# How v is loaded, how the last MLP group leaves, and who sets the order, in a fused attention and MLP kernel

## The chip, the cores and the metric

The kernel runs on one core of one Trainium2 chip. The core has a matrix engine (TensorE, PE in the profile; its weight loads are shown apart, as PEld), three engines for element work (VectorE or DVE, ScalarE or ACT, GpSimd or POOL), a SyncE (SP) that here only issues transfers, and 16 DMA engines. Each engine works through its own instructions strictly in the order in which they were written. ScalarE can issue transfers too, from a queue of its own. The metric is the device time of one execution, in microseconds (us); lower is better.

## The reference

```python
# q, k, v: (4 batches, 4 heads, 1088 tokens, 32);  S1, S2: (8, 32)
def phi(x):                               # 64 features of a token
    a = einsum('rd,bhsd->bhsr', S1, x);  b = einsum('rd,bhsd->bhsr', S2, x)
    return einsum('bhsi,bhsj->bhsij', a, b).reshape(..., 64)
kv  = einsum('bhsf,bhsd->bhfd', phi(k), v);   z = phi(k).sum(tokens)
att = einsum('bhsf,bhfd->bhsd', phi(q), kv) / (einsum('bhsf,bhf->bhs', phi(q), z) + 1e-6)
x   = att as 4352 tokens of 4 * 32 = 128 values
h   = x @ w_in                            # 128 -> 2048
out = (max(h, 0) + alpha * min(h, 0)) @ w_out    # 2048 -> 128, float32
```

## The kernel before

**Attention.** The 1088 tokens of a batch are taken so that partition-sized groups of 32 tokens have a stride of 34: token t * 34 + j stands in row t, block j, for 32 rows and 34 blocks. For keys and values the 34 blocks are dealt into four groups of at most nine that begin at blocks `K0 = (0, 9, 17, 25)`; group g sits on partitions 32g to 32g + 31 of `v_sb[b]`, and blocks that two groups share are left out of the later one (`w0 = g // 2`). One batch's v is loaded by four DMAs, one for each group (`l_v`, line 322): 32 partitions, all four heads, nine or eight blocks of 32 values.

For each batch, `keys` does: transpose k (L461), project it by S1 and S2 (L469, TensorE), transpose back (L476), multiply out the 64 features (L484, `phi`, four products, GpSimd or VectorE), the sum over tokens as a small Gram matrix (L499, then L506, L507 and L509) that goes into `Wq[b]` (L511), and the product with v (L519), copied (L523), transposed (L530) and copied (L532) into `kvw[b]`. L519 is the only reader of v.

Queries come in five units (`UNITS`): two for batch 0 (512 and 576 tokens), one for each other batch. A unit transposes q (L546), projects it and takes the denominator at once with `Wq[b]` (L555), transposes (L561), divides (L576 to L583), multiplies out the features (L590), transposes (L596), multiplies with `kvw[b]` (L610) and writes x, transposed and in bf16, to `xT` (L619).

**MLP.** `GROUPS` cuts the 4352 tokens into eight groups of 512 and a last one of 256. max(h, 0) + alpha * min(h, 0) is computed as (1 - alpha) * max(h, 0) + alpha * h, so that out = relu(h) @ ((1 - alpha) * w_out) + x @ W, with W = w_in @ (alpha * w_out), made once (transposes L430, scaling L438 or L441, products L448, copy L451). A group has 16 chunks: a product with `w_in` into a PSUM bank (L633), a relu into a buffer `rh` (L640 on ScalarE or L642 on VectorE), a product with `w_out` summed in PSUM bank O (L646); and one product with W (L653). The result stands by feature, tokens in columns; VectorE transposes it in blocks of 32 (L658), and four DMAs write 32 features each in runs of 128 bytes (L670). For the last group two of the four go out on ScalarE's queue.

**Order.** Each piece of work is an `op` with the engines that it may run on, an estimated duration, what it depends on and the buffers that it takes. At build time `schedule` picks, again and again, the ready op that its estimates let start first, ties by priority; `ORDER` overwrites the priorities of the first 200-odd ops. The order in which ops are picked is the order in which each engine runs. Where it expects TensorE to sit idle early on, it puts in products of zeros (`filler`, L382). Loads of batches 1 to 3 are held back by tiny writes on VectorE into the destination (`gate`, L356), after which SP may issue them.

SP issues at the start k0 (two DMAs), q0a, v0 (four), w_in (two), w_out (two). ScalarE issues S1 and S2 ("rows") and alpha, then loads its function table.

Of the kernel before, what the change touches and what calls it, by code (L numbers as in the profile page):

```python
# [12 lines left out]
BF16 = mybir.dt.bfloat16  # L13
# [15 lines left out]
SLACK = {"ACT": 140, "PE": 0, "DVE": 170}  # L29
# [3 lines left out]
ORDER = [  # L33
# [48 lines left out]
STICK = {"PE": 5000}  # L82


def schedule(ops, slots, filler=None):
# [4 lines left out]

    free_at = {"DVE": 830, "PE": 900, "POOL": 700, "ACT": 700}
    cfg, glued = "full", None
# [4 lines left out]
    def slot_free(s):  # L97
        h = holder[s]
        if h is None:
            return slot_at[s]  # L100
        if any(o.end is None for o in h.frees) or not h.frees:
            return None
        return max(o.end + 150 for o in h.frees)

    waits = {id(o): sum(d.end is None for d in o.deps) for o in ops}
    users = {}
    for o in ops:
        for d in o.deps:
            users.setdefault(id(d), []).append(o)
    ready = [o for o in ops if waits[id(o)] == 0]  # L110
    order = []
    while ready:
        best = None
        known = {}
        for o in ready:
            t0 = 0
            picks = []
            ok = True
            taken = set()
            for h in o.takes:  # L120
                for s in h.names:
                    if s not in known:
                        known[s] = slot_free(s)
                cand = sorted((known[s], s) for s in h.names if known[s] is not None and s not in taken)
                if len(cand) < h.n:
                    ok = False
                    break
                chosen = cand[:h.n]
                taken |= {s for _, s in chosen}
                picks.append([s for _, s in chosen])  # L130
                t0 = max([t0] + [t for t, _ in chosen])
            if not ok:
                continue
            for e, dur in o.eng.items():
                if e == "PE":
                    if glued is not None and o is not glued:
                        continue
                    if o.cfg != cfg:
                        dur += SWITCH
                    if free_at.get("PE", 0) < COLD and not o.warm:  # L140
                        dur *= 2
                t = max(t0, free_at.get(e, 0))
                if o.port and e in ("DVE", "POOL"):
                    t = max(t, free_at.get("PORT", 0))
                for d in o.deps:
                    t = max(t, d.end + (0 if d.on == e else d.lat if d.on == "DQ" else d.lat + SLACK.get(e, 0)))
                if e == "PE":
                    for i, (limit, at) in enumerate(have):
                        if issued + o.ni > limit:
                            t = max(t, have[i + 1][1])  # L150
                o_key = (t, o.prio, t + dur)
                if best is None:
                    best = []
                best.append((t, o.prio, t + dur, o, e, dur, picks))
        assert best, "no operation can start"

        t_first = min(b[0] for b in best)
        near = [b for b in best if b[0] <= t_first + 60]
        t, _, end, o, e, dur, picks = min(near, key=lambda b: (
            b[1] - (STICK["PE"] if b[4] == "PE" and b[3].cfg == cfg != "full" else 0), b[2]))  # L160
        if e == "PE" and filler and 4000 < free_at.get(e, 0) < FILL:
            each = 430 if free_at[e] < COLD else 215
            n = int((t - free_at[e] - 40) / each)
            idle = [s for s in FILL_BANKS if slot_free(s) is not None and slot_free(s) <= free_at[e]
                    and s not in sum(picks, [])]
            if n > 0 and idle:
                x = filler(n, idle[-1], each)
                x.behind = [f for f in holder[idle[-1]].frees] if holder[idle[-1]] else []
                x.end, x.on, x.took = free_at[e] + each * n, e, each * n
                order.append((free_at[e], e, x))  # L170
                slot_at[idle[-1]] = x.end
                holder[idle[-1]] = x.takes[0]
                issued += x.ni
                cfg = x.cfg
# [3 lines left out]
        if e == "PE":  # L178
            issued += o.ni
            cfg, glued = o.cfg, o.glue  # L180
            if issued > have[-1][0] - 256:
                have.append((have[-1][0] + 256, max(end, free_at.get("DQ", 0)) + 2600))
        for h, names in zip(o.takes, picks):
            h.got = names
            o.behind += [f for s in names if holder[s] for f in holder[s].frees]
            for s in names:
                holder[s] = h
        order.append((t, e, o))
        ready.remove(o)
        for u in users.get(id(o), ()):  # L190
            waits[id(u)] -= 1
            if waits[id(u)] == 0:
                ready.append(u)
# [5 lines left out]
def kernel(  # L199
# [12 lines left out]
    nc = tc.nc  # L212
# [511 lines left out]
```

## Time and profile before

| | us |
|---|---|
| median of three runs (105.97 to 108.0) | 106.73 |
| the profiled execution | 106.62 |
| its span, first to last instruction | 103.9 |
| TensorE busy in it | 96.5 |
| VectorE, ScalarE, GpSimd busy | 71.3, 71.3, 43.3 |
| first MLP product (L633) starts | 20.64 |
| last group's transpose (L658) starts | 100.18 |

A busy share is an average over the whole span, so the stages are looked at one by one: which engine a stage waits for last. In the lines of the timeline and of the groups stand the line of the code, the engine, the operation, the buffer written and those read, and how many instructions were taken together; times are microseconds from the span's start. In the chain that ended last, each piece is what released the next one. "SPq" and "ACTq" are the issuing of transfers by SP and ScalarE; "DMA" there is a transfer's way until it has landed. In a window's row stand, after its length, the busy times of PE, PEld, DVE, ACT and POOL with their instruction counts, the granted TensorE clock, the mean busy share of the 16 DMA engines and GB/s.

### The profile page before, as it was taken

What the parts mean: (1) busy time and instruction counts of PE and PEld (TensorE: products, weight loads), DVE (VectorE), ACT (ScalarE), POOL (GpSimd) and SP (SyncE); (2) the same over time, 40 slices, a digit from 0 to 9 for tenths busy, and PEclk for the clock granted to TensorE, in tenths of its full rate; (3) what the DMA queues carried; (4) which work ended last, traced back from release to release, by engine and by line L of the source; (5) the groups of instructions that cost most, each with busy time, mean ns of one, the idle gap of its engine ahead of it and who ended that gap; (6) DMA issues with size and microseconds to landing.
All of it is one profiled execution on the core that took longest, in us unless ns stands there. A gap on an engine that the chain in (4) does not pass through costs nothing.

```text
span 103.9 us, 3351 instructions
## 1 busy us (share of the span) xinstructions
PE 96.5 (93%) x1364; PEld 52.0 (50%) x1375; DVE 71.3 (69%) x154; ACT 71.3 (69%) x157; POOL 43.3 (42%) x47
## 2 busy tenths in 40 slices
PE   5978999999999999999999997999999999999950
PEld 4637789544653444446453444444444344444740
DVE  3556999997999994867867963892365544654740
ACT  1331998396676996664967952899798898694820
POOL 4009619499937999099159629700000000000000
PEclk9999999999999999999999999999999999999999
DMA  2999974965200777075002380140033060032243
GB/s 64 311 218 362 415 288 137 290 199 172 102 0 6 109 227 197 11 125 192 0 0 40 60 212 17 26 75 0 6 47 54 0 95 9 7 61 36 39 65 51
DMA packets 22863, 11.24 MB, mean 108 GB/s; under 512 B 19008, under 2 KB 21056, under 8 KB 22848
## 3 DMA queue, kind: packets, MB, share of 16 engines
q1 hardware_dynamic: 21952, 10.95, 40.5%
q8 instruction: 10, 0.16, 0.6%
q10 hardware_dynamic: 896, 0.08, 0.6%
q14 instruction: 5, 0.04, 0.1%
HBM read 8.80 MB, written 2.23 MB: 106 GB/s over the span
## 4 chain that ended last, share of the span: by engine, by line
PE 71%; DMA 8%; DVE 8%; SPq 6%; issue 3%; ACT 1%; ACTq 0%
PE O L646 24%; PE H L633 23%; SPq L305 6%; PE A L610 5%; DMA q_sb<-in_q_dram 5%; PE A L633 3%; DMA v_sb<-in_v_dram 3%; PE H L519 3%; PE O L448 3%; PE A L555 2%; DVE winT L438 2%; PE O L653 2%; PE A L469 1%; PE A L519 1%; PE A L499 1%
## 5 line engine op out<-in xcount | busy, mean ns | idle before, releaser
L640 ACT ACTIVATE rh<-H 128x512 bf16<-128x512 f32 (+1 forms) x96 | 50.8, 595 | 8.1 <-PE H L633 6.5
L633 PE MATMUL H<-xT,w_in_bf 128*128 128x512 bf16 (+1 forms) x122 | 40.0, 374 | 0.4 <-DVE ab L476 0.2
L646 PE MATMUL O<-rh,w_out_bf 128*128 128x512 bf16 (+1 forms) x135 | 39.8, 366 | 0.4 <-issue 0.2
L642 DVE TENSOR_SCALAR rh<-H 128x512 bf16<-128x512 f32 (+1 forms) x28 | 18.3, 658 | 7.1 <-PE H L633 5.9
L633 PEld LDWEIGHTS <-w_in_bf 128*128 128x128 bf16 x144 | 13.7, 99 | 16.4 <-issue 3.2
L484 POOL TENSOR_TENSOR phi<-ab 128x576 f32<-128x576 f32 x15 | 17.3, 1179 | 10.7 <-DVE ab L476 10.7
L646 PEld LDWEIGHTS <-w_out_bf 128*128 128x128 bf16 x144 | 13.9, 98 | 15.2 <-issue 1.7
L590 POOL TENSOR_TENSOR qf<-qa 128x1152 f32<-128x1152 f32 (+2 forms) x9 | 17.0, 1908 | 3.6 <-DVE qa L583 3.3
L658 DVE STREAM_TRANSPOSE oT<-O 128x512 f32<-128x512 f32 (+1 forms) x9 | 6.1, 683 | 9.6 <-PE O L646 7.1
L596 DVE STREAM_TRANSPOSE qp<-qf 128x1152 f32<-128x1152 f32 (+2 forms) x10 | 11.1, 1119 | 0.0
L561 DVE STREAM_TRANSPOSE qa<-A 128x288 f32<-128x288 f32 (+2 forms) x20 | 7.0, 395 | 2.2 <-PE A L555 2.2
L640 ACT ACTIVATE rh<-A 128x512 bf16<-128x512 f32 (+1 forms) x13 | 5.8, 514 | 2.6 <-PE A L633 2.5
L382 PE MATMUL O<-warm 128*128 128x256 bf16 x36 | 6.3, 338 | 1.1 <-DVE warm L364 1.1
L610 PE MATMUL A<-qp,kvw 32*32 32x288 f32 (+2 forms) x320 | 7.1, 364 | 0.0
L461 DVE STREAM_TRANSPOSE kT<-k_sb 128x544 f32<-128x544 f32 x8 | 5.6, 720 | 1.6 <-DMA k_sb<-in_k_dram 1.5
L619 ACT CAST xT<-A 128x128 bf16<-128x128 f32 (+3 forms) x12 | 3.3, 332 | 4.9 <-PE A L610 4.9
L412 ACT CAST w_in_bf<-w_in_f 128x512 bf16<-128x512 f32 x4 | 4.4, 1147 | 3.2 <-DMA w_in_f<-in_moe_w_in_dram 3.2
L546 DVE STREAM_TRANSPOSE qT<-q_sb 128x544 f32<-128x544 f32 (+2 forms) x10 | 5.7, 602 | 1.0 <-DMA q_sb<-in_q_dram 1.0
L583 POOL TENSOR_TENSOR qa<-qa,rd 128x288 f32<-128x288 f32 (+1 forms) x4 | 2.5, 630 | 8.6 <-DVE rd L582 6.3
L619 DVE CAST xT<-A 128x288 bf16<-128x288 f32 (+2 forms) x8 | 2.9, 392 | 3.7 <-PE A L610 3.7
L610 PEld LDWEIGHTS A<-qp,kvw 32*32 32x32 f32 x320 | 3.9, 103 | 2.8 <-issue 1.3
L382 PEld LDWEIGHTS <-warm 128*128 128x128 bf16 x36 | 4.1, 121 | 2.2 <-DVE warm L364 1.1
(80 smaller groups left out, 86.7 us busy)
## 6 DMA issues: line engine op xcount, KB each, us to landing
k_sb<-in_k_dram SPq DMA_DIRECT2D x3, 544.0 KB, 4.7
q_sb<-in_q_dram SPq DMA_DIRECT2D x3, 544.0 KB, 4.1
out_dram<-oT SPq DMA_DIRECT2D x20, 64.0 KB, 2.0
v_sb<-in_v_dram SPq DMA_DIRECT2D x8, 144.0 KB, 3.7
v_sb<-in_v_dram SPq DMA_DIRECT2D x8, 128.0 KB, 4.0
w_in_f<-in_moe_w_in_dram SPq DMA_DIRECT2D x2, 512.0 KB, 6.7
w_out_f<-in_moe_w_out_dram SPq DMA_DIRECT2D x2, 512.0 KB, 5.5
k_sb<-in_k_dram SPq DMA_DIRECT2D x2, 272.0 KB, 3.0
```

Of the source, the lines that this page charges most:

```text
L305: getattr(nc, eng).dma_start(dst, src)
L382: nc.tensor.matmul(bank[name][:, :256], warm[:, :128], warm[:, :256], start=True, stop=True)
L484: eng.tensor_mul(bufs[hph.got[0]][:, rr_, :, h2].rearrange("p w (i j) -> p w i j", i=r), view(src, [[64, KW], [1, r], [0, r]], 32 * rr_ + ...
L561: ta.append(op(("DVE", dve(n)), lambda h=h: nc.vector.transpose(bufs[hqa.got[0]][:, h * n:(h + 1) * n], bank[hA[h].got[0]][:, :n]), prio + ...
L590: side(e).tensor_mul(bufs[hqf[rr_].got[0]][:, :4 * n].rearrange("p (m i j) -> p m i j", i=r, j=r), view(src, [[32, 2 * nb], [1, r], [0, r] ...
L596: mu.append(op(("DVE", dve(4 * n) + 40), lambda rr_=rr_: nc.vector.transpose(bufs[hqp[rr_].got[0]][:, :4 * n], bufs[hqf[rr_].got[0]][:, :4 ...
L610: nc.tensor.matmul(bank[hX[c].got[0]][32 * h:32 * (h + 1), :n], kvw[b][32 * c:32 * (c + 1), i, 32 * h:32 * (h + 1)], view(bufs[hqp[h // 2] ...
L619: x_done[x0] = (w, op({"ACT": act(w), "DVE": dve(w)}, lambda e, c=c, w=w, x0=x0: copy(e)(xT[:, x0:x0 + w], bank[hX[c].got[0]][:, :w]), lat ...
L633: hm = op(("PE", n / 2.4 + 3), lambda c=c, hh=hh: nc.tensor.matmul(bank[hh.got[0]][:, :n], w_in_bf[:, c * 128:(c + 1) * 128], xT[:, col0:c ...
L640: nc.scalar.activation(bufs[hr.got[0]][:, :n], bank[hh.got[0]][:, :n], ACTF.Relu)
L642: nc.vector.tensor_scalar_max(bufs[hr.got[0]][:, :n], bank[hh.got[0]][:, :n], 0.0)
L646: nc.tensor.matmul(bank["O"][:, :n], w_out_bf[:, c], bufs[hr.got[0]][:, :n], start=state["n"] == 0, stop=state["n"] == last)
```

## The change

**v.** `K0` becomes (0, 9, 18, 25), so that the first three groups are 27 consecutive blocks. A batch's v is loaded by four DMAs, one for each head, that fill partitions 0 to 95: the DRAM side is read as 3 groups, 32 rows, 288 consecutive values. The fourth group (partitions 96 to 127, seven blocks) is a fifth DMA. For batch 0 ScalarE issues it after its table load, for the others SP issues it ahead of the four. The products that read v (L519) and the Gram products (L499) take 96 partitions for the first two blocks.

**The last group** (256 tokens) computes by token: the relu's buffer is the stationary operand in two halves of 128 tokens, `w_out` the moving one (128 columns), so its 17 products of 256 columns become 34 of 128, in two PSUM banks. From chunk 8 on the halves are separate ops. Each half is copied out by VectorE or ScalarE, without a transpose, and written by one DMA with runs of 512 bytes, one on SP's queue and one on ScalarE's; the DRAM side is 4 blocks, 32 rows, 128 values.

**The order.** `ORDER` and the picking are gone. `PLAN` lists all 720 ops by their number, in the order of issue, with a letter where an engine is to be chosen. The estimates are still used for choosing buffers and fillers. `rh` has 12 buffers instead of 10, and in the last group L633 may use bank O too. Read by engine, the beginning of the plan is: TensorE: warm-up, L389, L469, L499, L402, one block of L430, L509, L430, L555 (unit 0), two of L430, L519 (batch 0), L448 three times, L530, L448 four times, L610 (unit 0), L469 (batch 1), L448, two of L633, L555 (unit 1), L633 three times, L499 (batch 1), then 11 products of the first group, L509 among them, six more, L555 (unit 2), L519 (batch 1). VectorE has L511 of batch 0 ahead of one of the four `phi` products (after it before). The gate of v1 follows L476 of batch 1, that of v2 the first two L619 of unit 1, that of v3 L532 of batch 2. Batch 3's L519 comes in the third group's last third.

```diff
-    K0 = (0, 9, 17, 25)
+    K0 = (0, 9, 18, 25)
...
-    P_rh = pool("rh", 10, [128, 512], BF16)
+    P_rh = pool("rh", 12, [128, 512], BF16)
...
-    def l_v(b, g, eng="sync"):
-        w0 = g // 2
-        dma(eng, v_sb[b][32 * g:32 * (g + 1), :, w0:].rearrange("p h w d -> p h (w d)"),
-            dram(v, b * H * S * D + (K0[g] + w0) * D, [[NB * D, 32], [S * D, H], [1, (KW - w0) * D]]))
+    def l_v(b, h):
+        dma("sync", v_sb[b][:96, h].rearrange("p w d -> p (w d)"),
+            dram(v, (b * H + h) * S * D, [[KW * D, 3], [NB * D, 32], [1, KW * D]]))
+
+    def l_v3(b, eng):
+        dma(eng, v_sb[b][96:, :, 2:].rearrange("p h w d -> p h (w d)"),
+            dram(v, b * H * S * D + 3 * KW * D, [[NB * D, 32], [S * D, H], [1, (KW - 2) * D]]))
...
+    L["v0_"] = op(("ACT", 450), lambda: l_v3(0, "scalar"), -1980, lat=4500)
...
-    load("v0", 2700, lambda: [l_v(0, g) for g in (0, 2, 1, 3)])
+    load("v0", 1650, lambda: [l_v(0, h) for h in range(H)])
...
-        load(f"v{b}", 2600, lambda: [l_v(b, g) for g in (0, 2, 1, 3)], gate(v_sb[b][:1, 0, 0, :1], v_))
+        load(f"v{b}", 2300, lambda: [l_v3(b, "sync")] + [l_v(b, h) for h in range(H)], gate(v_sb[b][:1, 0, 0, :1], v_))
...
-                rows_ = slice(0, 64) if w == 0 else slice(0, 128)
+                rows_ = slice(0, 96) if w < 2 else slice(0, 128)
...
+        def by_token(i, x, w):
+            nc.tensor.matmul(bank[hT[i].got[0]][:, :DM], x, w, start=done[i] == 0, stop=done[i] == last)
+            done[i] += 1
...
+            def f_t(c=c, hr=hr, parts=(0, 1)):
+                for i in parts:
+                    by_token(i, bufs[hr.got[0]][:, 128 * i:128 * (i + 1)], w_out_bf[:, c])
...
+                ev = op({"DVE": dve(DM), "ACT": act(DM)}, lambda e, i=i, ho=ho: copy(e)(
+                    bufs[ho.got[0]][:, :4].rearrange("p a b -> p (a b)"), bank[hT[i].got[0]][:, :DM]),
+                    prio - 5, deps=os_ + ts, takes=[ho], frees=[hT[i]])
...
+                    dma(("sync", "scalar")[i], dram(out, (b * S + x // 32) * DM, [[DM, 4], [NB * DM, 32], [1, DM]]),
+                        bufs[ho.got[0]][:, :4].rearrange("p a b -> p (a b)"))
...
+def schedule(ops, slots, filler, plan):
...
+    for word in plan.split():
+        o = ops[int(word.rstrip("adp"))]
+        e = names[word[-1]] if word[-1] in names else next(iter(o.eng))
```

More of the change, by code (lines that the diff above doesn't have):

```diff
@@ L81 @@
 SWITCH, COLD, FILL = 95, 6600, 14000
[L82 to L92, printed above, removed]
+def schedule(ops, slots, filler, plan):
+    free_at = {"DVE": 830, "PE": 900, "POOL": 700, "ACT": 700, "SP": 0, "DQ": 0, "PORT": 0}
+    names = {"a": "ACT", "d": "DVE", "p": "POOL"}
+    cfg = "full"
     issued, have = 0, [(448, 0)]
@@ L102, in slot_free @@
             return None
[L103 to L107, printed above, removed]
-        for d in o.deps:
[L109 to L174, printed above, removed]
@@ L179, in schedule @@
             issued += o.ni
-            cfg, glued = o.cfg, o.glue
+            cfg = o.cfg
             if issued > have[-1][0] - 256:
[L182 to L186, printed above, removed]
+                have.append((have[-1][0] + 256, max(end, free_at["DQ"]) + 2600))
+        for h, got in zip(o.takes, picks):
+            h.got = got
+            o.behind += [f for s in got if holder[s] for f in holder[s].frees]
+            for s in got:
                 holder[s] = h
         order.append((t, e, o))
[L189 to L193, printed above, removed]
     assert all(o.end is not None for o in ops), "operations left"
@@ L395 @@
         Sk, view(ST, [[0, 2], [1, 2 * r]]), view(mask2, [[1, 2], [0, 2 * r]])), -870, deps=[c_st, c_mask])
-    c_wq = [op(("ACT", 150), lambda b=b: nc.scalar.copy(Wq[b][:, :2 * r], ST), -500 + b, deps=[c_st, c_w0[b]]) for b in range(B)]
+    c_wq = [op(("ACT", 150), lambda b=b: nc.scalar.copy(Wq[b][:, :2 * r], ST), -500 + b, deps=[c_st, c_w0[b], c_tab]) for b in range(B)]
     c_y = op(("DVE", 150), lambda: nc.vector.tensor_mul(
@@ L683 @@
         mlp(g, c0, n, 1000 * g, [x for s, (m, x) in x_done.items() if s < c0 + n and s + m > c0])
-    for o, x in zip(ops, ORDER):
-        o.prio = x
-    order = schedule(ops, slots, filler)
+    order = schedule(ops, slots, filler, PLAN)
     kernel.plan = order
```

115 lines of the change are left out of this document (100 added, 15 removed), and 15 rows, old and new, of the table ORDER.

## The prediction

> **What bounds the kernel now.** I read the page's head, then TensorE's busy time by stage, then the chain that ended last.
>
> ```profile
> span 103.9 us, 3351 instructions
> ...
> PEclk9999999999999999999999999999999999999999
> ```
>
> ```profile
> sum 84.00, PE 78.50 PEld 38.50 DVE 56.39 ACT 60.45 POOL 34.36; mean PE 8.72 PEld 4.28 DVE 6.27 ACT 6.72 POOL 3.82
> ```
>
> ```profile
> 17.93 0.34 PE O L448 x3
> 18.27 1.00 PE A L610 x56
> 19.27 0.65 PE H L469 x16
> 19.91 0.57 PE A L555 x30
> ...
> 20.64 0.38 PE H L633
> ...
> 51.57 1.29 PE O L646 x6
> ...
> 59.96 3.27 DMA v_sb<-in_v_dram
> ...
> 98.51 1.53 PE O L646 x14
> ...
> 100.18 0.45 DVE oT L658
> ```
>
> From 20.64 us, the first MLP matmul, to 100.18 us, where VectorE takes up the last result, TensorE is the limit: the windows from 20 to 104 hold 78.50 us of PE work, and as it ends at 100.18, some 1.6 us of idle time lie in the 80 before. One v load (v3, at 59.96) stands in the chain. A change can therefore move the start (20.64), the gaps (1.6 us) and the tail (100.18 to 103.9). TensorE's work between them stays, so any new wait in its queue is paid in full.
>
> **The v loads: how many DMA engines carry them.** This decides the sign, and I take it first.
>
> ```profile
> q1 hardware_dynamic: 21952, 10.95, 40.5%
> ...
> q10 hardware_dynamic: 896, 0.08, 0.6%
> ...
> out_dram<-oT ACTq DMA_DIRECT2D x2, 32.0 KB, 1.8
> rows<-in_S_dram ACTq DMA_DIRECT2D x2, 4.0 KB
> al<-in_moe_alpha_dram ACTq DMA_DIRECT2D x1, 8.0 KB, 5.9
> ```
>
> Count ScalarE's queue (q10). Two outputs of 32 KB in 128-byte rows are 512 packets, alpha in 32-byte rows 256, two "rows" loads of 4 KB in 128-byte rows 64: 832. The row says 896, so 64 more belong to five DMAs. On SP's queue the same count (five k and five q of 128 rows, sixteen v of 128, four weights of 128, 16,896 output rows) leaves 21952 - 20736 = 1216 over 76 DMAs, exactly 16 each. I read the extra as one closing packet for each engine that took part. Then alpha and the two outputs (outermost dimension 128 or 32) account for 48, and the two "rows" loads for 8 each; their outermost dimension is 8. So a DMA with a short outermost dimension ran on that many engines. The new head loads read DRAM as [3 groups][32 tokens][288 elements]: outermost 3. I expect 3 engines, where each old one used 16. The row outputs at the end have an outermost dimension of 4.
> The Trainium skill ("DMA: Bandwidth & Descriptors", section "Why a DMA increments its semaphore by 16 and not by 1") says the same as a rule: the largest count up to 16 that divides the outermost sizes of both sides, hence 3 for 3 and 96. The trace agrees with it at 8, 32 and 128; no run here shows 3. The same section also gives a 96-partition tile as an example of 16 engines, which would hold only if the DRAM side had 96 as well.
>
> Now the price of a packet. I took two windows of the DMA view: 61.2 to 63.02 us, where only v3 moves, and 8 to 13 us, where only the weights move.
>
> ```profile
> DMA packets 327, 0.31 MB, mean 169 GB/s; under 512 B 43, under 2 KB 327, under 8 KB 327
> ...
> q1 hardware_dynamic: 327, 0.31, 61.6%
> ...
> v_sb<-in_v_dram SPq DMA_DIRECT2D x2, 144.0 KB, 3.2
> ```
>
> ```profile
> q1 hardware_dynamic: 532, 1.95, 100.5%
> ```
>
> First: 0.616 x 16 x 1.82 us / 284 packets of data = 62 ns each with 16 engines active. Second: 1.005 x 16 x 5 us / 475 packets of 4 KB = 169 ns, or 47 ns for 1152 bytes at that rate. With only three engines drawing I take 50, ends 47 and 62. A batch's four head loads are 384 rows, 128 on each of three engines: 6.4 us (6.0 to 7.9). The old form put 32 on each of 16, 2.0 us. Both move the same bytes, and the last quarter (128 rows, outermost 32) stays cheap. Issue to landing was 3.2 us, of which 1.8 to 2.0 moved data, so I keep 1.4 us of latency.
>
> **Front.** SP issues k0, q0a, v0, then the weights, in both kernels.
>
> ```profile
> 9.18 1.59 DVE L484 TENSOR_TENSOR phi<-ab 128x576 f32<-128x576 f32 x1
> 9.62 0.29 PE L509 MATMUL A<-exs,G 128*128 128x8 f32 x2
> 10.05 1.16 PE L430 MATMUL H<-ident,w_in_f 128*128 128x128 f32 x8
> ...
> 12.01 0.70 DVE L561 STREAM_TRANSPOSE qa<-A 128x128 f32<-128x128 f32 x3
> 12.63 0.65 DVE L438 TENSOR_TENSOR winT<-H,al 128x512 f32<-128x512 f32 x1
> 13.54 0.29 DVE L576 TENSOR_TENSOR qa<-qa 128x128 f32<-128x128 f32 x1
> ...
> 15.22 0.69 DVE L590 TENSOR_TENSOR qf<-qa 128x512 f32<-128x512 f32 x1
> 16.82 0.06 DVE L356 MEMSET v_sb<- 1x1 f32 x1
> 16.87 0.71 DVE L596 STREAM_TRANSPOSE qp<-qf 128x512 f32<-128x512 f32 x1
> 18.20 1.07 PE L610 MATMUL A<-qp,kvw 32*32 32x128 f32 x64
> ```
>
> The weights queue behind v0 on the three engines: w_in's first half lands 6.4 - 2.0 = 4.4 us later (4.0 to 5.9 with the packet at 47 and 62), its reader L430 moves from 10.05 to 14.45. In the old order L509 (the z product of batch 0) ran at 9.62, ahead of L430. The written order puts the first L430 block in front of it. So L509 waits for a weight it doesn't use, and behind it stand Wq's last columns, L555 and the whole first query unit. From L430 at 14.45: a block of four transposes 0.58, L509 0.29, Wq's copy with its wait 0.35, the phi that the new order puts behind that copy on VectorE (0.7, at L590's rate with GpSimd idle; 1.59 beside it), winT 0.65, four L561 0.95, from L576 to the start of L590 1.68 (13.54 to 15.22), from L590 to the last L596 2.36 (15.22 to 17.58), 0.2 to TensorE. L610 starts at 22.2 instead of 18.20. MLP then begins 2.2 us later (L610 1.07, L469 0.65, four passes of L448 0.45), not 2.44, as the second unit's L555 moves behind two MLP matmuls: 24.4 for 20.64, **+3.8 us** (3.4 to 5.3). The fillers, v0's last quarter on ScalarE's queue (0.45 of issue, behind the first Wq copy), and Wq's and G's new place hide in this wait; without it the quarter would stand before w_in's first cast and cost at most 0.45.
>
> **v1 and v3.** Let N be L610's start.
>
> ```profile
> 19.95 0.85 DVE L476 STREAM_TRANSPOSE ab<-H 128x288 f32<-128x288 f32 x2 [0.22 <-PE H L469]
> 20.52 2.31 POOL L484 TENSOR_TENSOR phi<-ab 128x576 f32<-128x576 f32 x2 [1.53 <-DVE ab L476]
> ...
> 22.79 0.52 POOL L576 TENSOR_TENSOR qa<-qa 128x160 f32<-128x160 f32 x1
> ```
>
> The gate of v1 was at 16.82, before L610; it now stands on VectorE behind L476, which ended 2.6 us after N. With one quarter load's issue (0.5) ahead: N + 3.2 + 1.4 + 6.4 = N + 11.0. Batch 1's L519 is reached by TensorE at N + 2.2 plus 17 MLP matmuls at 0.215 (1.29 / 6; 3.7) and two L555, one L499 and one L509 (0.57 for the first of them, about 2.2 together, an estimate by their columns): N + 8.1; its phi products are ready at N + 7.8 (four at 1.16 and L576's 0.52). L519 waits **2.9 us**, and everything behind it in TensorE's queue with it (2.5 to 4.4).
> v3's gate follows the copy of batch 2's kvw; until batch 3's L519 stand 27 MLP matmuls, one L555 and one L499, 7.1 us, less 0.9 until the gate: 6.2 against 0.5 + 1.4 + 6.4 = 8.3: **2.1 us** (1.7 to 3.6). v2 has 10.8 us between and stays hidden; k3 queues behind v2 on the three engines, which may cost up to 1.5 (counted in the upper end alone).
>
> **Last group and tail.**
>
> ```profile
> 98.34 1.69 PE L646 MATMUL O<-rh,w_out_bf 128*128 128x256 bf16 x14
> ...
> 100.67 0.88 ACTq L305 DMA_DIRECT2D out_dram<-oT  x2
> ```
>
> ```profile
> 101.50:102.00 0.50, 0.00 (x0) 0.00 (x0) 0.00 (x0) 0.00 (x0) 0.00 (x0) 1.00 0.83 127
> 102.00:102.50 0.50, 0.00 (x0) 0.00 (x0) 0.00 (x0) 0.00 (x0) 0.00 (x0) 1.00 0.86 131
> ```
>
> ```profile
> L646 PEld LDWEIGHTS <-w_out_bf 128*128 128x128 bf16 x144 | 13.9, 98 | 15.2 <-issue 1.7
> ...
> L610 PEld LDWEIGHTS A<-qp,kvw 32*32 32x32 f32 x320 | 3.9, 103 | 2.8 <-issue 1.3
> ```
>
> 17 products of 256 columns at 0.109 (1.53 / 14) become 34 of 128, each with its own weights: 1.85 us if a load hides (0.054 each), 3.3 if the 98 ns load sets the pace. Loads of 32 columns last about as long (L610's 320 took 103 ns, while they started every 17), so duration is mostly latency: I take 66 ns, **+0.4** (0 to 1.5).
> The Trainium skill ("TensorE: Matmul & The Clock Gate", section "Back-to-back issue gap") gives about 81 ns for a stream of load and matmul at 128 columns; by that the term is an estimated +0.9.
> Tail: two copies of half the columns side by side for one transpose (L658's 0.45 against about 0.27, an estimate from L596's 0.71 and L561's 0.23 at 512 and 128 columns), one issue per queue for two (-0.44); the packets took 0.85 us, and 64 rows of 512 bytes on each of four engines take 1.3 at the weights' rate: **-0.2** (-1.1 on 16 engines, +0.5). Of the 1.6 us of gaps I let the written order and the deeper rh pool recover half, **-0.8** (0 to -1.6).
>
> **Sum** against the profiled execution's 106.62 (span 103.9 and 2.7 around it; the median, 106.73, is level): 3.8 + 2.9 + 2.1 + 0.4 - 0.2 - 0.8 = +8.2: **114.8 us**. Ends: the smallest waits (7.6) with every gain (2.7) give +4.9, 111.5; all upper ends together (13.3 of waits, k3 1.5, row products 1.5, tail 0.5) would give +16.8, but a longer front delays the reader of v1 no further, and I cut at 121.
>
> **Rivals.** *Sixteen engines.* If the DMA is spread by its 96 partitions, as all loads of before were by 32 or 128, the waits vanish: the chain above from 10.05, with phi at 1.59 beside GpSimd, ends at N = 18.7, MLP starts within 0.2 of 20.64, and gaps (-0.8), tail (-1.1), row products (+0.4) give -1.5: 105.1 us (103 to 107). For it: alpha's 128 partitions close on 16. Against it: the eight-row loads. The point is the outermost size of the DRAM side. This is also the case of a change that does what its words say. *Three engines, front only:* if v1's and v3's packets run faster or TensorE reaches L519 later than counted, 114.8 - 5.0 = 109.8 us (107 to 111.5). *Worse:* two idle stretches of over 3 us let the granted clock, 1.00 throughout before, fall, and k3 stalls too: above 121.
>
> **How the numbers follow.** Forecast 0.58, front only 0.15, sixteen engines 0.22, worse 0.05. The range, 106 to 121, holds the first two and three tenths of the third (0.58 + 0.15 + 0.07). Around the median a measurement tells 2%, 104.6 to 108.9: faster 0.09 and same 0.11 from sixteen engines, 0.03 more from front only, a remnant of 0.02 slower; slower 0.77 in all.
>
> **What would show it.** Right: v head loads land 8 us after issue or more, DMA share near 3/16 while they move alone; L430 waits for w_in until about 14.5; PE L519 waits for v_sb twice or more, some 5 us together. Closing packets on SP's queue fall to 3 per head load. Wrong: L519 released by POOL or by nothing, L430 near 10, v landing in 4 us.

## The result and the profile after

The changed kernel takes 126.32 us (median of four runs, 125.86 to 127.31) against 106.59 us for the kernel before beside it: a ratio of 1.189, 95% interval 1.178 to 1.199. Slower was right, and so was the place; the size was not. The forecast was 114.8 with a range up to 121. Some executions of a kernel take over 1.5% longer than its fastest; the ratios leave them out. The profiled execution took 127.31 us, the longest of the four; its span is 125.3.

In the changed kernel the lines have moved: L430 is L412, L509 is L491, L519 is L501, L610 is L592, L469 is L451, L555 is L537 (all 18 lower), L633 is L621 and L646 is L634 (12 lower); L615 holds the new row products, L660 their copies. First its page: head, granted clock, the two queues that carry the change, and the new head loads.

```profile
span 125.3 us, 3392 instructions
...
PEclk9999559999985699999999756999999999999999
...
q1 hardware_dynamic: 21252, 10.83, 33.3%
q10 hardware_dynamic: 628, 0.20, 0.7%
...
v_sb<-in_v_dram SPq DMA_DIRECT2D x16, 108.0 KB
```

Two things answer to the lines of before. The clock, a row of nines then, falls three times. And the closing packets come out as read: on q10, 64 packets of "rows", 256 of alpha, 128 of v's last quarter and 128 of row output make 576, and the 52 that are left are 8 + 8 + 16 + 16 + 4. The row output ran on four engines.

Where the time went is read from the waits (engine, bank, line, what released it: us in all, times, the longest) and from the chain that ended last, both of the changed kernel.

```profile
PE H L412 <- DMA w_in_f<-in_moe_w_in_dram: 6.5, 1, 6.5
...
PE H L501 <- DMA v_sb<-in_v_dram: 3.7, 3, 1.7
...
PE A L501 <- DMA v_sb<-in_v_dram: 2.8, 3, 1.3
...
PE H L451 <- DVE kT L443: 1.1, 1, 1.1
```

```profile
5.34 10.05 DMA w_in_f<-in_moe_w_in_dram
15.43 1.12 PE H L412 x4
...
24.55 1.00 PE A L592 x56
...
29.49 7.61 DMA v_sb<-in_v_dram
37.14 2.13 PE H L501 x66
...
48.72 7.11 DMA k_sb<-in_k_dram
...
56.73 1.34 PE H L451 x16
...
64.41 7.22 DMA v_sb<-in_v_dram
71.67 2.13 PE A L501 x66
```

TensorE now waits for w_in, for v1, for k3 and for v3: four transfers of 7 to 10 us are on the path where, behind q's first load (4.93), one of 3.27 was. The windows of the same trace show a second loss (columns as before: length, busy PE, PEld, DVE, ACT, POOL, granted clock, DMA share, GB/s).

```profile
9.00:15.40 6.40, 0.00 (x0) 0.00 (x0) 0.49 (x3) 0.27 (x1) 1.93 (x3) 0.77 0.91 272
15.40:20.00 4.60, 4.57 (x65) 3.74 (x68) 2.94 (x10) 2.79 (x8) 0.00 (x0) 0.58 0.39 109
32.56:39.27 6.71, 3.00 (x84) 2.37 (x74) 3.52 (x9) 0.78 (x3) 3.20 (x4) 0.78 0.57 183
39.27:46.00 6.73, 6.73 (x82) 3.04 (x83) 1.59 (x6) 4.09 (x10) 2.18 (x2) 0.71 0.01 3
70.00:75.00 5.00, 3.60 (x72) 2.47 (x73) 0.20 (x1) 0.99 (x3) 3.28 (x2) 0.55 0.54 92
75.00:80.00 5.00, 5.00 (x49) 2.20 (x48) 2.46 (x4) 3.01 (x7) 0.00 (x0) 0.77 0.00 1
```

Behind each wait TensorE is busy again, but in rows with a mean clock of 0.55 to 0.78. Busy time times the missing clock, an estimate of what that costs, is 1.9 us in the second row and 0.66 + 1.95 + 1.62 + 1.15 = 5.4 us in the last four.

The span grew by 21.4 us. The first MLP product (L621) starts at 26.67 for 20.64: 6.0. From there to TensorE's end, 93.6 us for 79.5: 14.1, of which 6.0 is idle time (7.6 for 1.6), 5.4 the clock, 0.6 the unit of L555 that was moved behind the MLP's start, and some 2 us that this trace does not assign; the run with zeros, below, puts most of them down to the clock too. From TensorE's end to the end of the span, 5.1 for 3.7: 1.3.

### The profile page after: what moved, and what is told of

Read it like the earlier page. It is cut to its first block, busy times and chain, and to the rows that moved or that the text cites. A ratio compares the mean times of both kernels' runs of the same rounds, so it can differ in the third digit from the quotient of the medians.

```text
span 125.3 us, 3392 instructions
## 1 busy us (share of the span) xinstructions
PE 104.8 (84%) x1388; PEld 56.8 (45%) x1388; DVE 74.8 (60%) x162; ACT 70.9 (57%) x156; POOL 42.8 (34%) x47
## 3 DMA queue, kind: packets, MB, share of 16 engines
q1 hardware_dynamic: 21252, 10.83, 33.3%
## 4 chain that ended last, share of the span: by engine, by line
PE 59%; DMA 26%; SPq 7%; DVE 2%; issue 1%; ACT 0%; DVEq 0%
PE O L634 18%; PE H L621 16%; DMA v_sb<-in_v_dram 12%; DMA w_in_f<-in_moe_w_in_dram 8%; SPq L281 7%; DMA k_sb<-in_k_dram 6%; PE A L592 4%; PE O L430 3%; PE A L501 3%; PE H L501 3%; PE A L621 3%; PE H L412 2%; PE H L451 2%; PE A L615 2%; PE A L537 1%
## 5 line engine op out<-in xcount | busy, mean ns | idle before, releaser
L628 ACT ACTIVATE rh<-H 128x512 bf16<-128x512 f32 (+1 forms) x90 | 49.1, 589 | 17.7 <-PE H L621 17.0
L621 PE MATMUL H<-xT,w_in_bf 128*128 128x512 bf16 (+1 forms) x125 | 41.4, 389 | 0.0
L634 PE MATMUL O<-rh,w_out_bf 128*128 128x512 bf16 x128 | 40.3, 394 | 0.0
L630 DVE TENSOR_SCALAR rh<-H 128x512 bf16<-128x512 f32 (+1 forms) x35 | 22.3, 650 | 7.6 <-PE H L621 7.2
L466 POOL TENSOR_TENSOR phi<-ab 128x576 f32<-128x576 f32 x15 | 17.3, 1173 | 14.2 <-DVE ab L458 14.2
L621 PEld LDWEIGHTS <-w_in_bf 128*128 128x128 bf16 x144 | 13.8, 100 | 16.9 <-issue 4.3
L634 PEld LDWEIGHTS <-w_out_bf 128*128 128x128 bf16 x128 | 13.0, 102 | 15.5 <-issue 3.2
L677 DVE STREAM_TRANSPOSE oT<-O 128x512 f32<-128x512 f32 x8 | 5.6, 706 | 8.9 <-PE O L634 8.9
L412 PE MATMUL H<-ident,w_in_f 128*128 128x128 f32 x12 | 2.9, 382 | 6.5 <-DMA w_in_f<-in_moe_w_in_dram 6.5
L501 PE MATMUL H<-phi,v_sb 128*32 128x64 f32 (+1 forms) x144 | 4.2, 263 | 3.7 <-DMA v_sb<-in_v_dram 3.7
L592 PE MATMUL A<-qp,kvw 32*32 32x288 f32 (+2 forms) x320 | 7.1, 364 | 0.0
L564 DVE RECIPROCAL rd<-rd 128x36 f32<-128x36 f32 (+2 forms) x5 | 1.6, 324 | 9.1 <-ACT rd L562 9.1
L501 PE MATMUL A<-phi,v_sb 128*32 128x64 f32 (+1 forms) x144 | 4.3, 263 | 2.8 <-DMA v_sb<-in_v_dram 2.8
L558 POOL TENSOR_TENSOR qa<-qa 128x288 f32<-128x288 f32 (+1 forms) x4 | 2.9, 724 | 10.5 <-DVE qa L543 10.5
L621 PE MATMUL A<-xT,w_in_bf 128*128 128x512 bf16 (+1 forms) x18 | 5.7, 338 | 0.0
```

What stands on the lines that cost most here:

```text
L466: eng.tensor_mul(bufs[hph.got[0]][:, rr_, :, h2].rearrange("p w (i j) -> p w i j", i=r), view(src, [[64, KW], [1, r], [0, r]], 32 * rr_ + ...
L501: nc.tensor.matmul(bank[hK.got[0]][32 * h:32 * (h + 1), :R], v_sb[b][rows_, h, w], bufs[hph.got[0]][rows_, h // 2, w, h % 2], start=(w == ...
L592: nc.tensor.matmul(bank[hX[c].got[0]][32 * h:32 * (h + 1), :n], kvw[b][32 * c:32 * (c + 1), i, 32 * h:32 * (h + 1)], view(bufs[hqp[h // 2] ...
L621: hm = op(("PE", n / 2.4 + 3), lambda c=c, hh=hh: nc.tensor.matmul(bank[hh.got[0]][:, :n], w_in_bf[:, c * 128:(c + 1) * 128], xT[:, col0:c ...
L628: nc.scalar.activation(bufs[hr.got[0]][:, :n], bank[hh.got[0]][:, :n], ACTF.Relu)
L630: nc.vector.tensor_scalar_max(bufs[hr.got[0]][:, :n], bank[hh.got[0]][:, :n], 0.0)
```

## The experiments

Twelve kernels ran. The kernel before ran beside them on the same chips, with medians of 106.45 to 106.61 us. A time below is the median of all runs; a difference to the kernel before is worked out from the ratio (the ratio less one, times 106.2 us), and is good to about 1 us. By it the change costs 20.0 us.

### Is it the number of engines?

The changed kernel with everything kept but the split of v's 96 partitions: three DMAs of 32 partitions with the 32 rows outermost, for four with the 3 groups outermost. Bytes and packets of data are the same.

```diff
-    def l_v(b, h):
-        dma("sync", v_sb[b][:96, h].rearrange("p w d -> p (w d)"),
-            dram(v, (b * H + h) * S * D, [[KW * D, 3], [NB * D, 32], [1, KW * D]]))
+    def l_v(b, g):
+        dma("sync", v_sb[b][32 * g:32 * (g + 1)].rearrange("p h w d -> p h (w d)"),
+            dram(v, b * H * S * D + g * KW * D, [[NB * D, 32], [S * D, H], [1, KW * D]]))
```

> The changed kernel with one thing undone: partitions 0 to 95 of v are loaded by three DMAs of 32 partitions and all four heads (outermost dimension 32 on both sides) in place of four head loads (outermost 3 in DRAM). Layout, bytes, written order, gates and the row output stay. Theory (three engines): v lands within 4 us of its issue, the L412 reader of w_in starts near 10 us instead of 15.4, none of the L501 products waits for v for more than 0.5 us, the clock stays 1.00; about 105 us (102 to 108). Rival (the written order, which puts the weight's transposes ahead of the z product and the gates of v1 and v3 late, makes the waits whatever carries v): 118 us or more.

105.61 us (104.83 to 106.84), ratio 0.993 (0.989 to 0.998). No wait of TensorE for v is left, L412 waits 0.5 us for w_in, and the MLP starts at 20.34. The page of this kernel:

```profile
q1 hardware_dynamic: 21396, 10.83, 41.2%
```

144 packets more than in the changed kernel: 12 loads with 16 closing packets each (192) for 16 loads with 3 each (48). The data packets did not change, so the count of engines is shown, and the rival, the written order, falls. A stretch in which nothing but head loads moves shows the same from the other side. The DMA view of the changed kernel from 29.6 to 31.2 us (q1: packets, MB, share of 16 engines):

```profile
DMA packets 95, 0.11 MB, mean 71 GB/s; under 512 B 3, under 2 KB 94, under 8 KB 94
...
q1 hardware_dynamic: 94, 0.10, 19.3%
```

19.3% of 16 engines is 3.1 engines, and 0.193 x 16 x 1.6 us / 94 packets is 53 ns a packet, against the 50 that I took. The Trainium skill ("DMA: Bandwidth & Descriptors", section "Why a DMA increments its semaphore by 16 and not by 1") has the rule for both counts, the largest number up to 16 that divides the outermost sizes of both sides; the runs agree with it now at 3 and at 4 too.

The other way round, the kernel before, in its own order, with nothing but the new loads:

```diff
-    K0 = (0, 9, 17, 25)
+    K0 = (0, 9, 18, 25)
...
-    load("v0", 2700, lambda: [l_v(0, g) for g in (0, 2, 1, 3)])
+    load("v0", 2700, lambda: [l_v(0, h) for h in range(H)] + [l_v3(0, "sync")])
...
-        load(f"v{b}", 2600, lambda: [l_v(b, g) for g in (0, 2, 1, 3)], gate(v_sb[b][:1, 0, 0, :1], v_))
+        load(f"v{b}", 2600, lambda: [l_v3(b, "sync")] + [l_v(b, h) for h in range(H)], gate(v_sb[b][:1, 0, 0, :1], v_))
...
-                rows_ = slice(0, 64) if w == 0 else slice(0, 128)
+                rows_ = slice(0, 96) if w < 2 else slice(0, 128)
```

> The kernel before with the new way of loading v alone (groups at 0, 9, 18, 25; four head loads on partitions 0 to 95 and one of the last quarter, all on SP's queue); its own order, gates and output by feature. Theory (three engines): w_in some 5 us later at the front, batch 3's product waits some 5 us, batch 1's and 2's little since their gates come early; 116 us (111 to 121). Rival (the written order makes the loss): below 109 us.

121.01 us (120.33 to 121.63), ratio 1.138 (1.130 to 1.145), at the upper end of the expected range; the mean granted clock of its profiled execution was 0.94. Its waits (here L434 and L523 are before's L430 and L519):

```profile
PE H L434 <- DMA w_in_f<-in_moe_w_in_dram: 6.0, 1, 6.0
PE H L523 <- DMA v_sb<-in_v_dram: 4.5, 4, 1.4
...
PE A L523 <- DMA v_sb<-in_v_dram: 1.2, 1, 1.2
```

The same waits without the written order: the loads alone cost 14.6 us. With them the written order and the new last group cost another 5.4 (20.0 - 14.6).

### What does the slow clock cost?

The changed kernel with added work: 58, 48 and 44 products of zeros on TensorE ahead of the first weight transposes and of batch 1's and batch 3's kv products, so that it never idles for w_in or v.

```diff
         def f_wt(i=i, hb=hb):
+            if i == 0:
+                zeros(29, hb.got[0])
...
         def kvm(w0, w1):
+            if b in (1, 3):
+                zeros({1: 24, 3: 22}[b], hK.got[0])
```

> The changed kernel, with products of zeros on TensorE where it would sit idle: 58 of 256 columns ahead of the first block of weight transposes (6.2 us), 48 ahead of batch 1's L501 and 44 ahead of batch 3's (5.1 and 4.7 us). Transfers and order are untouched. Theory (each wait costs a second time, because the granted clock falls behind it): v and w_in land when they did, the clock stays at 1.00 behind the waits, 119 to 122 us. Rival (only the waits themselves count): 125 to 128 us.

121.44 us (121.14 to 122.0), ratio 1.143 (1.136 to 1.149): 4.9 us less than the changed kernel (give or take 1.4), with more work in it. Two rows of its windows, and its clock on the page:

```profile
9.00:15.40 6.40, 6.40 (x61) 5.77 (x60) 0.38 (x3) 0.83 (x2) 1.83 (x3) 1.00 0.87 270
15.40:20.00 4.60, 4.60 (x131) 4.07 (x130) 3.93 (x14) 4.10 (x15) 0.32 (x1) 1.00 0.54 174
```

```profile
PEclk9999999999999999999999999999999999999996
```

L592 starts at 22.42 here, for 24.48. No wait of TensorE for v or w_in is left in this run, and the zeros took longer than the waits that they fill, which hides some of the gain: from the MLP's start to TensorE's end (24.70 to 114.94) TensorE was busy for 89.1 us, 10.3 of them with zeros, where the changed kernel idled 6.5 us for v. That leaves 78.9 us of its own work, for 85.9 in the changed kernel and 78.0 in the kernel before. The 7.0 us between are an estimate of what the slow clock costs behind the MLP's start, more than the 5.4 of the windows; at the front, from L412's start to L592, it is 1.7 (7.4 us for 9.1). So the slow clock costs at least 4.9 us, by the traces nearer to 9, and the wait itself is not the whole price of a late load.

### Which of the late stretches costs what?

Batch 0's v by group as above, batches 1 to 3 by head.

```diff
-    load("v0", 1650, lambda: [l_v(0, h) for h in range(H)])
+    load("v0", 1650, lambda: [l_vg(0, g) for g in (0, 2, 1)])
```

> The changed kernel, with batch 0's v loaded as three DMAs of 32 partitions (outermost 32, all DMA engines) and batches 1 to 3 by head as before. Theory (each of the waits is paid by itself): the front is cured, the first weight transposes (L412) start near 10, the first L592 near 18.2 and the MLP near 20.4, 6.2 us earlier than in the changed kernel; the waits of batch 1's and batch 3's kv products for v, k3 behind v2, and the fall of the granted clock behind them stay: 119.5 to 120.5 us. Rival (the late front is what makes the later loads late, and most of the loss comes from it): 112 us or less, and at most one wait for v left.

118.41 us (117.02 to 119.63), ratio 1.112 (1.100 to 1.123): 8.2 us less than the change (7.9 by the medians), a little more than expected. The MLP starts at 19.81. The waits for v are as long as in the changed kernel (here L506 is L501):

```profile
PE H L506 <- DMA v_sb<-in_v_dram: 4.1, 3, 1.7
...
PE A L506 <- DMA v_sb<-in_v_dram: 3.0, 3, 1.3
```

So the front and the later waits are separate losses, and the rival, that the front is most of it, falls.

The later waits were to be taken away by earlier issue. Three kernels failed at that, for a reason of mine. In the written order I put batch 1's gate and load behind w_out's loads (ops 79, 80), and batch 3's k and v around batch 2's v (121, 122 and 125, 126), and dropped what the gates depend on:

```diff
-        load(f"k{b}", 1600, lambda: l_k(b), gate(k_sb[b][:1, :1], k_))
+        load(f"k{b}", 1600, lambda: l_k(b), gate(k_sb[b][:1, :1], *([] if b in EARLY_K else [k_])))
...
-        load(f"v{b}", 2300, lambda: [l_v3(b, "sync")] + [l_v(b, h) for h in range(H)], gate(v_sb[b][:1, 0, 0, :1], v_))
+        load(f"v{b}", 2300, lambda: [l_v3(b, "sync")] + [l_v(b, h) for h in range(H)],
+             gate(v_sb[b][:1, 0, 0, :1], *([] if b in EARLY_V else [v_])))
...
-    49 43d 50 10 147 148
+    49 43d 50 10 79 80 147 148
...
-    330 112 103 343
+    330 112 121 122 103 125 126 343
```

> The changed kernel, batch 1's v issued right behind the weights (its gate waits for nothing), everything else as it is: its 384 packets move from about 15.5 to 22 while TensorE transposes the weights. Theory (the wait of batch 1's kv products for v and the slow clock behind it have a price of their own): no wait for batch 1's v, TensorE at full clock from the MLP's start on; 4.6 us of wait, 0.9 of slow kv products and about 1.9 of slow clock behind them go: 119 to 121 us. Rival (batch 1's v only hides work that is late anyway, another wait takes its place): 124 or more.

125.36 us (124.65 to 126.55), ratio 1.177 (1.169 to 1.184). The wait moved. A gate is an instruction of VectorE, and at that place in its order it stood behind the scaled copies of the transposed weights, which wait for w_in: v1's head loads were issued from 18.7 on, k1 behind them, and in the timeline of this kernel TensorE waits for k1's transpose (L452 is L451):

```profile
29.70 1.88 PE L452 MATMUL H<-kT,Sk 64*32 64x288 f32 x16 [4.71 <-DVE q_sb L338]
```

> The changed kernel, with k of batch 3 issued ahead of v of batch 2, and v of batch 3 right behind it: the same loads in another order and without the gates of k and v of batch 3. Theory: no wait for k of batch 3 (1.1), none for v of batch 3 (3.4 with its slow kv products), no slow clock behind them (about 2): 119 to 121 us. Rival (v of batch 2, later by one k load on the three engines, becomes late itself): a wait for v of batch 2, 124 or more.

127.67 us (127.36 to 128.22), ratio 1.201 (1.195 to 1.207). The gate of k3 stood late on VectorE, SP reached v2 at 51.45, and batch 2's kv products, which never waited before, wait for v2:

```profile
PE A L502 <- DMA v_sb<-in_v_dram: 3.3, 3, 1.1
```

> Both of these at once: of the three late stretches only the front is left. Theory (the prices add up; batch 0's v by group alone gave 7.9 us): 113 to 114.5 us, which is 105.6 (all v loads by group) and the front's 7.9. Rival (the front's delay is worth its 6 us on the clock of the trace and no more): 111.6 or less; rival (the later waits overlap): 116 or more.

128.5 us (128.26 to 128.68), ratio 1.209 (1.202 to 1.215): both displaced waits in one kernel. In the first two the rivals came true; the third reached its rival's time, but by the displaced waits and not by an overlap. They say nothing yet on the price of the waits, but show how it is with such loads: what is issued next to one is held up (with v1 early, k1 was issued at 20.97 and was there at 28.87, 7.9 us later, where the k loads of the kernel before took 4.7, their median). The last kernel has the same loads, with the gates at the start of VectorE's order:

```diff
-    14 11 13 19 20 3 57
+    14 11 13 19 79 121 125 20 3 57
...
-    50 10 147 148
+    50 10 80 147 148
...
-    330 112 103 343
+    330 112 122 103 126 343
```

> As the last of the three runs with early loads, but with the three gates (one memset each) at the very start of VectorE's order, where they wait for nothing; in those runs the gates stood behind VectorE's work of the late stretch, so that v of batch 1 was issued at 18.7 us and not near 8, and v of batch 2 at 51 and not near 45. Here v of batch 1 should be issued before 9 us, k of batch 3 near 34 and v of batch 3 right behind v of batch 2, near 49. Theory (each late stretch has its own price, and only the front is left): no wait of TensorE for v of batches 1 and 3 and for k of batch 3, 112.5 to 115 us. Rival (three engines have no room: each load that is moved up makes another one late, as k of batch 1 behind v of batch 1 did): a wait of over 2 us for k of batch 1 or v of batch 2, 119 or more.

115.98 us (115.06 to 116.62), ratio 1.090 (1.076 to 1.103), 10.5 us less than the change, and just above the theory's 112.5 to 115. No wait for v or k3 is left. One wait for k1 behind v1 is, which the theory had put at nothing:

```profile
27.53 1.88 PE L452 MATMUL H<-kT,Sk 64*32 64x288 f32 x16 [1.95 <-DVE q_sb L338]
```

It costs more than its 1.95: the products behind it ran slowly too (a mean clock of 0.76 from 24.51 to 30.35), and the MLP starts at 30.35, 3.7 us after the changed kernel's. From there to TensorE's end it is 78.6 us, for 78.1 with all v loads by group, so the later waits are gone whole. The parts then are: front 8.2, later waits 10.5, together 18.7 of the 20.7 that all v loads by group are worth (20.0 + 0.7). Without the new wait for k1 the later ones would be worth up to 14.2, an estimate; the two parts would then add up to 22.4, and the difference to 20.7 lies within what runs of this spread can tell.

### Does the z product carry the front?

The changed kernel with its head loads and another written order: the z product (op 68, L491), its copy, one `phi`, and VectorE's chain of the first query unit ahead of the first weight transposes (33 40 41a 42).

```diff
-    30 144 145 33 40 41a 67 68 42 69d 63d 74 8 9 146
+    30 144 145 67 68 69d 63d 74 146 147 148 150 149 151 152 153 154 155 33 40 41a 42 8 9
...
-    50 10 147 148 150 149 151 152 153 154 155 158d
+    50 10 158d
```

> The changed kernel with its head loads, and only the written order changed at the front: the z product of batch 0, its copy, phi on VectorE, unit 0's z multiplication and VectorE's chain of the first query unit stand ahead of the first weight transposes, which wait for w_in. Theory (the prediction's step: the z product waits for a weight that it doesn't use): the first L592 starts at 20.7 to 22.5 instead of 24.5, the whole at 123 to 125 us. Rival (the weights' own chain, w_in, transposes, Wq and its products, sets the start of L592): L592 stays at 24 or later and the whole at 126.

124.13 us (123.05 to 126.02), ratio 1.163 (1.155 to 1.171). The total fell into the theory's band, its mechanism did not carry it. From the timeline of this kernel, of an execution that took 124.96 us:

```profile
9.67 0.36 PE L491 MATMUL A<-exs,G 128*128 128x8 f32 x2 [0.27 <-DVE exs L489]
...
15.23 2.82 PE L412 MATMUL H<-ident,w_in_f 128*128 128x128 f32 x12 [4.31 <-DMA w_in_f<-in_moe_w_in_dram]
...
18.83 1.46 PE L501 MATMUL A<-phi,v_sb 96*32 96x64 f32 x72
20.22 1.60 PE L430 MATMUL H<-w_out_f,winT 128*128 128x128 f32 x12
...
23.76 1.07 PE L592 MATMUL A<-qp,kvw 32*32 32x128 f32 x64
```

The z product is done at 10, yet L592 starts at 23.76, 0.7 us earlier than in the changed kernel and near the rival's 24. The weight products that stand ahead of it on TensorE (L430) begin at 20.22, and the MLP starts at 26.14 for 26.67. By the ratio this order is worth 2.7 us; what goes beyond that 0.5 lies behind the MLP's start, and this run doesn't say where it is from.

### The last group and the tail

The kernel before, in its own order and with its own loads, with only the last group by token as rows: `by_token` and `f_t` of the change, a copy of 128 columns for each half, outermost dimension 4 in DRAM.

```diff
+            def f_t(c=c, hr=hr, parts=(0, 1)):
+                for i in parts:
+                    by_token(i, bufs[hr.got[0]][:, 128 * i:128 * (i + 1)], w_out_bf[:, c])
...
+                    dma(("sync", "scalar")[i], dram(out, (b * S + x // 32) * DM, [[DM, 4], [NB * DM, 32], [1, DM]]),
```

> The kernel before with one part of the change: its last MLP group's output by token as rows, outermost dimension 4; loads and scheduler as before. Theory (the row products cost nothing, the row output runs on 4 engines and takes about 2 us where the old one took 0.85, but has one issue fewer and half the copies): 0.0 to +0.8 us, 106.5 to 107.3; 25 or more row products back to back at 0.056 us each. Rival (each row product waits for its own weight load, 0.098 us): +1.5 us on top, 108 or more. Rival of my prediction's tail term: -0.2.

107.83 us (107.11 to 108.91), ratio 1.015 (1.008 to 1.022): +1.6, above both my tail term and this expectation. In its chain (L633 are the row products, L648 relus):

```profile
100.05 0.42 DVE rh L648
...
100.52 0.44 DVE rh L648
...
101.46 0.46 PE A L633 x8
```

The products cost what was expected, 0.06 us each, 8 in 0.46. What wasn't counted are two relus that the last ones wait for, 0.9 us.

Then the same with 32 outermost: `xT` keeps the last 256 tokens in another order, so that one row of the product is one partition of the output's 32.

```diff
+                if m < w:
+                    copy(e)(view(xT, [[128, 2], [1, 4], [4, 32]], x0 + m),
+                            bank[hX[c].got[0]][:, m:w].rearrange("p (i j t) -> p i j t", i=2, j=4))
...
-                    dma(("sync", "scalar")[i], dram(out, (b * S + x // 32) * DM, [[DM, 4], [NB * DM, 32], [1, DM]]),
+                    dma(("sync", "scalar")[i], dram(out, (b * S + x // 32) * DM, [[NB * DM, 32], [DM, 4], [1, DM]]),
```

> As the run of rows at the end alone, but xT keeps the last 256 tokens in another order, so that the output's DRAM side begins with 32 instead of 4. Theory (the engines that carry the output are the whole difference): packets in 0.7 us instead of 2, 1.0 to 1.5 us less than with outermost 4, 105.0 to 105.7. Rival (the end is set by the latency from issue to landing, not by packets): no difference between the two.

106.64 us (105.81 to 108.58), ratio 1.005 (1.000 to 1.010), +0.5: 1.1 us below the run with 4, as expected of the engines. The level is 0.9 above what I wrote. The chain of this kernel has one relu ahead of the last row products, which is half of that; where the other half is from isn't shown.

```profile
99.43 0.44 DVE rh L653
```

Both edits, v by group and 32 outermost, in the changed kernel:

> The same as e1_v_by_group, and the last 256 tokens stand in xT so that a half's result has row 4t + j: the DRAM side of the two row outputs is then 32, 4, 128 (outermost 32) in place of 4, 32, 128. One more small copy in batch 3's L601. Theory (a DMA runs on as many engines as its outermost dimension allows): the last packets take 0.5 us instead of 1.9, and the kernel is 1.0 to 1.4 us shorter than e1_v_by_group. Rival (issue and landing latency set the end, not the packets): within 0.3 us of it.

104.32 us (103.65 to 106.34), ratio 0.980 (0.973 to 0.987). This version beats both kernels, the one before by 1.3 to 2.7%. Two rows show the tail, a window of the changed kernel and one of this one, while almost only the row outputs move:

```profile
122.50:123.00 0.50, 0.00 (x0) 0.00 (x0) 0.00 (x0) 0.00 (x0) 0.00 (x0) 1.00 0.28 84
```

```profile
100.20:101.00 0.80, 0.00 (x0) 0.00 (x0) 0.00 (x0) 0.00 (x0) 0.00 (x0) 1.00 0.69 178
```

84 GB/s with a quarter of the engines, 178 with all (131 KB in 0.8 us would be 164, the rest are last packets of the group before). The output packets took 0.74 us (100.23 to 100.96) for 1.9 in the changed kernel (121.97 to 123.88).

These four kernels make a square. With 4 outermost, written order and group loads stand at -0.7 us, before's order and loads at +1.6; with 32 outermost at -2.1 and +0.5. So the output's engines are worth 1.1 to 1.4 us in either order, and the order, with the split of v that came with it and the deeper `rh`, 2.3 to 2.6. On top of the head loads the same order, with the new last group, costs 5.4 us.

## Why the prediction was wrong

**Three engines: right, and shown.** The read-out of closing packets held at 3 and 4, and with it the sign. The rival of sixteen engines fell, and so did the one of the front only, with the waits for v1 and v3. Sixteen engines had 105.1 us, near the 105.61 with all v loads by group, but by luck: that number has the output on sixteen engines as well, and the run with both took 104.32.

**Packets: 50 ns was right, 6.4 us a batch was not.** Alone a packet takes 53 ns; but a batch's packets were spread from 28.79 to 36.26, 7.5 us for 128 on an engine (58 ns), while SP took 2.99 us for the four issues and loads issued behind them shared the engines. (The upper end of 62 ns comes out at 63 from its own numbers.)

```profile
27.20 2.99 SPq L281 DMA_DIRECT2D v_sb<-in_v_dram  x4
```

**Front: +3.8 predicted, +6.0 measured.** Two things failed, the start of w_in's reader and the clock behind it. The reader started at 15.43, not 14.45, as SP's longer issues for v0 put w_in's own at 5.34, for 4.2 before; this was not in the sum. From there to L592 I counted 7.7 us at full clock; it took 9.1. With the clock held up by zeros it took 7.4 (15.02 to 22.42). So the chain was counted well for a clock that it didn't have: in 15.4 to 20 us the clock was 0.58, straight behind 6.4 us of idle time. What I made carry the front, the z product held up by a weight, is worth 0.7 us in the one trace that has it earlier; there the weights' own products set the start of L592.

**v1: +2.9 predicted, 4.6 measured.** TensorE reached L501 at N + 8.08 (32.56 us; predicted 8.1) and went on at 37.14; 3.7 us of that were idle. v was complete at N + 12.6 for 11.0: 7.5 us of packets for 6.4, and half a microsecond more of issue and landing. The 66 products behind it took 2.13 us where batch 0's 72 took 1.15.

**k3 and v3.** k3 stood at nothing in the sum and waited 1.1, behind v2 as feared in the upper end. v3's reader was reached at 68.01 and went on at 71.67: 3.7 us for 2.1, 2.8 of them idle.

**The clock: the step that failed.** The sum counts the work behind each wait at full clock; the slow clock stands in it at nothing. It is what the rival "worse" named and priced at 0.05; the time landed in it. I had the row that should have raised it, a front wait of 4.4 us in my own sum, and counted every later duration at a clock of 1.00 all the same. It costs at least 4.9 us (zeros in the waits); by the traces an estimated 1.7 at the front and 7.0 behind the MLP's start (5.4 by the windows). My condition, two idle stretches of over 3 us, was also too strict: at v3 TensorE was never idle for over 1.3 us at a time, three times in 3.4 us with two products between each, and the clock over the 5 us from 70 on was 0.55.
The Trainium skill ("TensorE: Matmul & The Clock Gate", section "What's actually happening") has a clock of one half after an idle window of about 3.4 us, and full clock after as long a busy one. The front agrees: 6.4 us of idle time, then 0.58 over 4.6 us. The wait for v3 differs if the rule is read as one unbroken gap.

**Row products: +0.4 predicted, 0 measured.** The chain of the changed kernel:

```profile
118.83 1.41 PE A L615 x25
...
120.27 0.27 ACT oT L660
```

25 products of 128 columns, each with its own weights, took 1.41 us: 0.056 each, the lower end that I gave. By the Trainium skill's 81 ns (same page, section "Back-to-back issue gap") they would have taken an estimated 2.0; the measurement decides.

**Tail: -0.2 predicted, +1.3 measured.** The copies took 0.27 and 0.29, as estimated, one issue went; but four engines moved the output in 1.9 us, not 1.3, and ScalarE's issue took 0.65.

**Gaps: -0.8 predicted.** Not to be read in the changed kernel. With the loads cured TensorE ends at 98.45 for 100.16, so the order with what came along was worth more, 1.7.

Together, on the span: front 2.2 too little, from the MLP's start to TensorE's end 9.5 too little (14.1 for 2.9 + 2.1 + 0.4 - 0.8), tail 1.5. Of the 9.5, an estimated 7.0 are the clock, and 1.8 are idle time: 6.0 where waits less gaps were to give 4.2. The waits were sized a little short; what a wait does to the work behind it was left out.

## What to carry to other kernels

Read the outermost size of both sides of a DMA before anything else: a nicer-looking access pattern with 3 or 4 in front ran on 3 or 4 of 16 engines, and the same bytes with 32 in front turned +20.0 us into -0.7. When a sum contains a wait of TensorE, ask at what clock the work behind it will run; here it was 0.55 to 0.78, and that cost about as much as the idle time itself (an estimated 7.0 us beside 7.6, from the MLP's start on). And a load on few engines is not cured by issuing it earlier, unless the load behind it has time to spare.

## What the runs showed of the hardware

- The closing packets of a queue give the engines of its DMAs: 21396 - 21252 = 12 x 16 - 16 x 3.
- SP took 0.70 us to issue a head load on three engines, and 0.43 a load of 32 partitions on sixteen (medians, the changed kernel and v by group).
- TensorE's clock was 0.55 over 5 us behind three waits of at most 1.3 us each, with two products between each (68.3 to 71.7 us of the changed kernel).
- A fresh 128 x 128 bf16 weight load for each product of 128 columns was free: 0.056 us a pair, 25 in a row.
